# Two 2 KB vectors loaded as one descriptor each, with one-row matmuls making their columns, in a single-core decode step

## The chip, the cores and the metric

The kernel runs on one core of one Trainium2 chip. The metric is the device time of one execution in microseconds (us). Before the change it was 440.36 us, the median of three runs (440.32 to 440.46). Profiles are of one execution each. Where this text says "the profile", "the trace", "the timeline" or "the windows", it means views of such an execution. PE is the matmul engine, DVE the vector engine, ACT the scalar engine, POOL the GpSimd engine and SP the engine that issues most loads.

## The reference, cut to what matters

The reference is one decode step: adaLN modulation from `c`, attention of 32 query heads over a cache of 4 key heads and 65,536 positions, and a gated feed-forward block.

```python
mod = (silu(c) @ w_mod).reshape(1, 6, 1, 1024)        # c: (1, 1024), w_mod: (1024, 6144)
sa, ca, ga, sb, cb, gb = (mod[:, i] for i in range(6))
h = layernorm(x) * (1 + ca) + sa                      # x: (1, 1, 1024)
x = x + ga * attention(h, k_cache, v_cache, wq, wo)   # caches: (1, 4, 65536, 128) each
h = layernorm(x) * (1 + cb) + sb
x = x + gb * ((gelu(h @ w_gate) * (h @ w_up)) @ w_down)
```

All data is bf16. The weights and caches are 185.6 MB. The two vectors `c` and `x`, which the change is about, are 2 KB each.

## The kernel before

SP streams the weights and caches through ten slots of SBUF, the on-chip memory that the engines compute from. (PSUM, below, is the memory that PE writes its results to.) A descriptor is one contiguous piece of a load. In the trace each descriptor is a packet, and each of the 16 DMA engines that takes part in a load adds a packet of 4 bytes at its end, the completion. Before the change, ACT's queue loads `c` and `x` at the start. Each is wanted as columns, element `8 p + k` in partition `p`, so each load has 128 descriptors of 16 bytes. `x` is loaded a second time as eight rows of 256 bytes, which one matmul turns into a second column layout, `x_nat`.

```python
def emit_all():
    act.dma_start(c_in[:, :], c[0].rearrange("(p k) -> p k", p=P)).then_inc(c_sem, 16)
    act.dma_start(x_in[:, :], A_x[0, 0].rearrange("(p k) -> p k", p=P)).then_inc(x_sem, 16)
    act.dma_start(x_row[:, :], A_x[0, 0].rearrange("(j p) -> j p", p=P)).then_inc(in_sem, 16)
    # ... (cut) SP issues w_mod (8 loads), wq (4), then keys, values and the other weights
    # ... (cut) POOL: identities, small fills, and then the large one:
    v_zero = GP.done(pool.memset(kt_sb[:, 1, :, :], 0.0))
    # ... (cut) DVE: fills of s_pad, h_pad, o_pad
    AC.wait((c_sem, 16))
    v_th = AC.done(act.activation(th_col[:, :], c_in[:, :], ACT.Tanh, scale=0.5))
    DVE.wait(v_th)
    v = DVE.done(dve.tensor_scalar(sg_col[:, :], th_col[:, :], 0.5, 0.5, ALU.mult, ALU.add))
    DVE.wait(v, v_pads, (c_sem, 16))
    v_s = DVE.done(dve.tensor_tensor(s_pad[:, :, 0], c_in[:, :], sg_col[:, :], ALU.mult))   # silu(c)
    # ... (cut) PE: the layernorm's sums, then w_mod against s_pad, chunk by chunk
```

## Time and profile before

| | before |
|---|---|
| median time | 440.36 us |
| DMA: bytes, mean rate | 185.89 MB, 424 GB/s |
| PE busy, share of the span | 80% |
| packets on the queue of `c` and `x` | 304 |
| `s_pad` (silu of `c`) ready | 12.0 us |
| first w_mod matmul | 12.86 us |

The first lines are from the page of the kernel before: the busy share of the DMA engines in 40 equal slices, in tenths, what they moved, and the packets by queue. Queue q1 is SP's, q10 is ACT's.

```profile
DMA  8999999999999999999999999999999999999995
GB/s 332 427 435 428 430 429 432 432 433 425 430 445 420 453 414 455 408 445 438 410 448 415 445 419 442 427 435 432 430 437 424 439 423 433 432 427 431 424 425 237
DMA packets 11957, 185.89 MB, mean 424 GB/s; under 512 B 1568, under 2 KB 1568, under 8 KB 1952
...
q1 hardware_dynamic: 11632, 185.61, 98.8%
...
q10 hardware_dynamic: 304, 0.01, 0.0%
...
DMA 60%; PE 35%; DVE 2%; issue 1%; SPq 1%; ACT 1%; POOL 0%
```

The DMA engines are busy in 8 or 9 tenths of every slice but the last, and the rate stays between 408 and 455 GB/s except in the first slice and the last. The last line is the chain of waits by engine: 60% is DMA. So the span is a start, a stream at a fixed rate, and a tail. The 304 packets of q10 (264 descriptors and 40 completions; the 272 in the prediction below is a slip) carry 0.01 MB, and their recorded time rounds to 0.0% of the span.

The next lines are from the timeline before: start in us, duration in us, engine, line, operation, output and inputs, and in brackets the idle time before and what ended it.

```profile
4.75 6.95 POOL L341 MEMSET kt_sb<- 128x8192 bf16 x1
...
6.69 5.03 DVE L356 TENSOR_SCALAR sg_col<-th_col 128x8 f32<-128x8 f32 x1
...
11.76 0.20 DVE L358 TENSOR_TENSOR s_pad<-c_in,sg_col 128x8 bf16<-128x8 bf16 x1
...
12.86 4.78 PE L392 MATMUL kt_ps<-slots,s_pad 128*32 128x512 bf16 x36
...
18.16 1.04 PE L392 MATMUL kt_ps<-slots,s_pad 128*32 128x512 bf16 x12 [0.52 <-DMA slots<-in_w_mod_dram]
...
433.51 2.91 PE L372 MATMUL b<-u_col,slots 128*128 128x1 bf16 x96 [3.01 <-DMA slots<-in_B_w_down_dram]
```

`sg_col` has 8 elements in each partition and takes 5.03 us, until POOL's memset ends at 11.70 us. It ends with the memset and not with the landing of `c`, whose tanh had started at 5.01 us. PE then works off three w_mod chunks (36 matmuls) without a wait. At 18.16 us it waits for DMA for the first time, and it does so for each later chunk.

### The profile page before, as it was taken

The page shows a single profiled execution, that of the slowest core. Times are in us where ns is not written, and L with a number is a line of the kernel's source. Part 1 is how long each engine was busy: PE and PEld are TensorE (multiplying, and loading weights), DVE is VectorE, ACT ScalarE, POOL GpSimd, SP SyncE. Part 2 cuts the span into 40 slices and gives each one's busy share as a digit, 9 for nine tenths or more (in the row PEclk, how much of TensorE's full clock was granted, in tenths as well). Part 3 has the DMA queues.
Part 4 walks back from the last instruction along what each step waited for, and adds up shares of the span by engine and source line. Part 5 has one row for each costly group of instructions (what it writes and reads, how often), then busy time and mean ns, then how long its engine had stood idle before and what let it go on. Part 6 is the DMA issues. An engine that isn't in the chain of part 4 may idle for free.

```text
span 438.8 us, 15336 instructions
## 1 busy us (share of the span) xinstructions
PE 351.7 (80%) x7107; PEld 318.4 (73%) x7107; DVE 176.2 (40%) x300; ACT 146.4 (33%) x553; POOL 11.7 (3%) x25
## 2 busy tenths in 40 slices
PE   0547449998989889898799989999989999557554
PEld 0214139998989879798799989899988999434234
DVE  4102013545444644455444466345563365142100
ACT  1000001343435634344613553444654434600000
POOL 8100000000000000000000000000000000000000
PEclk9955555959777986869955899556995597659855
DMA  8999999999999999999999999999999999999995
GB/s 332 427 435 428 430 429 432 432 433 425 430 445 420 453 414 455 408 445 438 410 448 415 445 419 442 427 435 432 430 437 424 439 423 433 432 427 431 424 425 237
DMA packets 11957, 185.89 MB, mean 424 GB/s; under 512 B 1568, under 2 KB 1568, under 8 KB 1952
## 3 DMA queue, kind: packets, MB, share of 16 engines
q1 hardware_dynamic: 11632, 185.61, 98.8%
q8 instruction: 13, 0.21, 0.2%
q10 hardware_dynamic: 304, 0.01, 0.0%
q14 instruction: 8, 0.07, 0.0%
HBM read 185.60 MB, written 0.00 MB: 423 GB/s over the span
## 4 chain that ended last, share of the span: by engine, by line
DMA 60%; PE 35%; DVE 2%; issue 1%; SPq 1%; ACT 1%; POOL 0%
DMA slots<-in_A_v_cache_dram 39%; PE kt_ps L561 18%; DMA slots<-in_A_k_cache_dram 10%; DMA slots<-in_B_w_down_dram 7%; PE b L625 7%; PE sc_ps L581 6%; DMA slots<-in_w_mod_dram 4%; PE kt_ps L392 2%; PE b L605 1%; SPq L234 1%; PE b L372 1%; ACT p_sb L691 1%; PE b L595 1%; DVE kt_sb L751 0%; PE sc_ps L453 0%
## 5 line engine op out<-in xcount | busy, mean ns | idle before, releaser
L561 PE MATMUL kt_ps<-ident,slots 128*128 128x128 bf16 x2048 | 179.5, 258 | 11.0 <-DMA slots<-in_A_k_cache_dram 10.3
L561 PEld LDWEIGHTS kt_ps<-ident,slots 128*128 128x128 bf16 x2048 | 154.9, 118 | 12.7 <-issue 9.8
L660 DVE COPY kt_sb<-kt_ps 128x2048 bf16<-128x2048 bf16 x96 | 117.6, 1225 | 108.6 <-PE kt_ps L561 108.5
L660 ACT ACTIVATE kt_sb<-kt_ps 128x2048 bf16<-128x2048 bf16 x32 | 60.1, 1877 | 183.3 <-PE kt_ps L561 183.3
L625 PE MATMUL b<-p_sb,slots 128*128 128x8 bf16 x2176 | 75.8, 168 | 20.6 <-DMA slots<-in_A_v_cache_dram 11.2
L625 PEld LDWEIGHTS b<-p_sb,slots 128*128 128x128 bf16 x2176 | 69.8, 100 | 23.3 <-DMA slots<-in_A_v_cache_dram 12.3
L691 ACT ACTIVATE p_sb<-sc_ps,mneg 128x64 bf16<-128x64 f32 x256 | 83.5, 560 | 3.9 <-DVE mneg L686 3.9
L691 ACT ACTIVATION_READ_ACCUMULATOR p_sb<-sc_ps,mneg 128x1 f32 x256 | 77.1, 365 | 0.0
L581 PE MATMUL sc_ps<-q_buf,kt_sb 128*128 128x8 bf16 x2112 | 69.9, 167 | 0.5 <-issue 0.5
L581 PEld LDWEIGHTS sc_ps<-q_buf,kt_sb 128*128 128x128 bf16 x2112 | 67.9, 100 | 0.6 <-issue 0.6
L392 PE MATMUL kt_ps<-slots,h_pad 128*32 128x512 bf16 x176 | 17.1, 510 | 14.3 <-DMA slots<-in_A_wq_dram 6.3
L684 DVE TENSOR_REDUCE mg<-b 8x1 f32<-8x128 f32 x32 | 8.9, 279 | 37.1 <-PE b L595 37.1
L679 DVE TENSOR_REDUCE m_col<-sc_ps 128x8 f32<-128x512 f32 x32 | 21.8, 681 | 4.7 <-PE sc_ps L581 4.7
L392 PEld LDWEIGHTS kt_ps<-slots,h_pad 128*32 128x32 bf16 x176 | 5.0, 112 | 24.1 <-DMA slots<-in_A_wq_dram 8.3
L392 PE MATMUL kt_ps<-slots,s_pad 128*32 128x512 bf16 x96 | 12.5, 553 | 9.3 <-DMA slots<-in_w_mod_dram 9.3
L392 PEld LDWEIGHTS kt_ps<-slots,s_pad 128*32 128x32 bf16 x96 | 3.6, 119 | 17.3 <-DMA slots<-in_w_mod_dram 12.6
L605 PE MATMUL b<-negi,mg 8*128 8x8 f32 x66 | 15.8, 309 | 0.0
L605 PEld LDWEIGHTS b<-negi,mg 8*128 8x128 f32 x66 | 12.7, 239 | 2.2
L453 PEld LDWEIGHTS sc_ps<-identf,kt_sb 128*128 128x128 f32 (+1 forms) x48 | 7.6, 204 | 8.2 <-DVE kt_sb L774 4.3
L453 PE MATMUL sc_ps<-identf,kt_sb 128*128 128x128 f32 (+1 forms) x48 | 9.1, 352 | 4.5 <-DVE kt_sb L774 2.4
L686 DVE COPY mneg<-b 128x8 f32<-128x8 f32 x32 | 5.3, 167 | 18.1 <-PE b L605 18.1
L372 PE MATMUL b<-u_col,slots 128*128 128x1 bf16 x224 | 6.6, 165 | 6.5 <-DMA slots<-in_B_w_down_dram 5.9
(97 smaller groups left out, 84.9 us busy)
## 6 DMA issues: line engine op xcount, KB each, us to landing
slots<-in_A_k_cache_dram SPq DMA_DIRECT2D x16, 4096.0 KB, 20.3
slots<-in_A_v_cache_dram SPq DMA_DIRECT2D x32, 2048.0 KB, 26.5
slots<-in_w_mod_dram SPq DMA_DIRECT2D x8, 1536.0 KB, 17.5
slots<-in_A_wq_dram SPq DMA_DIRECT2D x4, 2048.0 KB, 35.2
slots<-in_A_wo_dram SPq DMA_DIRECT2D x4, 2048.0 KB, 32.5
slots<-in_B_w_gate_dram SPq DMA_DIRECT2D x4, 1792.0 KB, 21.9
slots<-in_B_w_up_dram SPq DMA_DIRECT2D x4, 1792.0 KB, 23.6
slots<-in_B_w_down_dram SPq DMA_DIRECT2D x3, 2048.0 KB, 29.1
```

Of the source, the lines that this page charges most:

```text
L372: ins = pe.matmul(bank[:, j:j + 1], view[:, kk, j * P:(j + 1) * P], rhs[:, k0 + kk:k0 + kk + 1], start=first, stop=True, skip_group_check= ...
L392: ins = pe.matmul(out, pad[:, k, :], jb.view[:, kk, c0:c0 + ROW], start=k <= last_k[0], stop=k >= last_k[1], skip_group_check=True,)
L453: ins = pe.transpose(dst[:, i * w:i * w + n], src[:, a], identf[0:src.shape[0], 0:n])
L561: ins = pe.transpose(kt_ps[:, half * 2048 + t * P:half * 2048 + (t + 1) * P], j_k[i - i % KU].view[:, i % KU * CH + b * TB + t, :], ident[ ...
L581: ins = pe.matmul(sc_ps[:, base + n * REP:base + (n + 1) * REP], kt_sb[:, j % 2, n, :], q_buf[:, j % SITES, :], start=True, stop=True,)
L605: ins = pe.matmul(b6[:, 256:256 + REP], mg8[:, j % 2:j % 2 + 1].to_broadcast([REP, P]), negi[:, :], start=True, stop=True,)
L625: ins = pe.matmul(b7[:, s * REP:(s + 1) * REP], j_v[j].view[:, n, :], p_sb[:, s, n, :], start=(n == 0), stop=(n == CH - 1),)
L660: ev[i % SITES][b].done(act.activation(dst, src, ACT.Copy) if E_ is AC else dve.tensor_copy(dst, src))
L679: m1[s].done(dve.tensor_reduce(m_col[:, j % 2, :].unsqueeze(2), scv, AX.X, ALU.max))
L684: m2[s].done(dve.tensor_reduce(mg8[:, j % 2:j % 2 + 1], b6[0:REP, 32:32 + P], AX.X, ALU.max))
L686: v_mc[j] = DVE.done(dve.tensor_copy(mneg[:, j, :], b6[:, 256:256 + REP]))
L691: ins = act.activation(p_sb[:, s, :, h], scv[:, h, :], ACT.Exp, bias=mneg[:, j, h:h + 1], scale=scale, accum_out=z_all[:, j, h:h + 1],)
```

## The change

The intent is to get rid of 256 descriptors of 16 bytes (and eight of 256 bytes) in the first microseconds. `c` and `x` come as one row each in a single partition, one 2 KB descriptor each. Matmuls with a contraction of one row turn strided slices of that row into columns in PSUM, and DVE copies them out.

```diff
-        act.dma_start(c_in[:, :], c[0].rearrange("(p k) -> p k", p=P)).then_inc(c_sem, 16)
-        act.dma_start(x_in[:, :], A_x[0, 0].rearrange("(p k) -> p k", p=P)).then_inc(x_sem, 16)
-        act.dma_start(x_row[:, :], A_x[0, 0].rearrange("(j p) -> j p", p=P)).then_inc(in_sem, 16)
+        act.dma_start(c_row, c).then_inc(c_sem, 16)
+        act.dma_start(x_row, A_x[0]).then_inc(x_sem, 16)
 ... (cut)
-        AC.wait((c_sem, 16))
-        v_th = AC.done(act.activation(th_col[:, :], c_in[:, :], ACT.Tanh, scale=0.5))
+        PE.wait(t1, (c_sem, 16))
+        for j in range(KD):
+            ins = pe.matmul(b7[:, j:j + 1], c_row[:, j:D:KD], ident[0:1, 0:1], start=True, stop=True)
+        v_cp = PE.done(ins)
+        PE.wait((x_sem, 16))
+        for j in range(KD):
+            pe.matmul(b6[:, j:j + 1], x_row[:, j:D:KD], ident[0:1, 0:1], start=True, stop=True)
+            ins = pe.matmul(
+                b6[:, KD + j:KD + j + 1], x_row[:, j * P:(j + 1) * P], ident[0:1, 0:1], start=True, stop=True)
+        v_xp = PE.done(ins)
+        DVE.wait(v_cp)
+        v_c = DVE.done(dve.tensor_copy(c_col[:, :], b7[:, 0:KD]))
+        AC.wait(v_c)
+        v_th = AC.done(act.activation(th_col[:, :], c_col[:, :], ACT.Tanh, scale=0.5))
+        DVE.wait(v_xp)
+        v_x = DVE.done(dve.tensor_copy(x_col[:, :], b6[:, 0:KD]))
+        v_x = DVE.done(dve.tensor_copy(x_nat[:, :], b6[:, KD:2 * KD]))
 ... (cut: sg_col as before; s_pad reads c_col in place of c_in; the old x_row matmul and x_nat copy go)
```

The rows lie in a part of `kt_sb` that nothing else uses until w_mod is done.

More of the change, by code (lines that the diff above doesn't have):

```diff
@@ L120, in bass_adaLN_cond__gqa_block_cached__geglu_ffn__decode_kernel @@
     sp, pe, dve, act, pool = nc.sync, nc.tensor, nc.vector, nc.scalar, nc.gpsimd
-    in_sem = nc.alloc_semaphore("in_sem")
     c_sem = nc.alloc_semaphore("c_sem")
@@ L138, in bass_adaLN_cond__gqa_block_cached__geglu_ffn__decode_kernel @@
     halfneg = sb("halfneg", [P, 1])
-    x_row = sb("x_row", [KD, P], dt.bfloat16)
-    c_in = sb("c_in", [P, KD], dt.bfloat16)
-    x_in = sb("x_in", [P, KD], dt.bfloat16)
+    c_col = sb("c_col", [P, KD])
     s_pad = sb("s_pad", [P, KD, QD], dt.bfloat16)
@@ L175, in bass_adaLN_cond__gqa_block_cached__geglu_ffn__decode_kernel @@
     row_m = ktf(0)[:, 0:4 * ROW]
+    c_row = kt_sb[0:1, 0, 0:KD, :].rearrange("p a b -> p (a b)")
+    x_row = kt_sb[0:1, 0, KD:2 * KD, :].rearrange("p a b -> p (a b)")
     row_q = ktf(0)[:, 4 * ROW:6 * ROW]
@@ L352, in emit_all @@
             v_pads = DVE.done(dve.memset(a[:, :, :], 0.0))
-        AC.wait((c_sem, 16))
-        v_th = AC.done(act.activation(th_col[:, :], c_in[:, :], ACT.Tanh, scale=0.5))
+        PE.wait(t1, (c_sem, 16))
[15 more added lines that the diff above has]
+        v_x = DVE.done(dve.tensor_copy(x_nat[:, :], b6[:, KD:2 * KD]))
         DVE.wait(v_th)
         v = DVE.done(dve.tensor_scalar(sg_col[:, :], th_col[:, :], 0.5, 0.5, ALU.mult, ALU.add))
-        DVE.wait(v, v_pads, (c_sem, 16))
-        v_s = DVE.done(dve.tensor_tensor(s_pad[:, :, 0], c_in[:, :], sg_col[:, :], ALU.mult))
-        DVE.wait((x_sem, 16))
-        v_x = DVE.done(dve.tensor_copy(x_col[:, :], x_in[:, :]))
+        DVE.wait(v, v_pads)
+        v_s = DVE.done(dve.tensor_tensor(s_pad[:, :, 0], c_col[:, :], sg_col[:, :], ALU.mult))
         def col_matvec(bank, jobs, rhs, ready, nblk):
@@ L460, in quads @@
             return t.rearrange("p (n g y) -> p n g y", n=n, g=w // QD)[:, :, :, 0]
-        PE.wait(t1, (in_sem, 16))
-        v_xt = PE.done(pe.matmul(b6[:, 0:KD], x_row[:, :], ident[0:KD, 0:KD], start=True, stop=True))
         hn1, v_hn1 = ln_norm(x_col[:, :], v_x, 16)
@@ L503, in rest_of_mod @@
             dve.tensor_copy(ga_nat[:, :], nv[:, 0, :])
-            dve.tensor_copy(gb_nat[:, :], nv[:, 1, :])
-            DVE.wait(v_xt)
-            DVE.done(dve.tensor_copy(x_nat[:, :], b6[:, 0:KD]))
+            DVE.done(dve.tensor_copy(gb_nat[:, :], nv[:, 1, :]))
         def place_2(b0, n):
```

## The prediction

> **What bounds the kernel now.** The DMA engines. The page shows a DMA share of 9 tenths or more in every slice but the first and last, 185.9 MB at a mean of 424 GB/s; in 5 us windows the rate stays near 430 GB/s from 3 to 430 us. Issue to landing takes 20 to 35 us (DMA issues), so the queue always holds several MB. The chain of waits is 60% DMA. PE is second (80% busy, mean granted clock 0.73), but what it releases late only shortens a long backlog. So time = start-up + bytes / rate + tail. Bytes and tail (last w_down chunk at 433.5 us, then about 5 us) don't change.
>
> **What the change removes.** The queue of c and x has 304 packets: 272 descriptors and completions. In the first 32 us they take 0.5% of the 16 engines: about 0.16 us of the stream. The windows agree: about 420 GB/s from 3 to 12 us, with these packets, against about 427 GB/s from 12 to 20 us, which is 0.15 us. The ramp (124, 222, 246 GB/s in the half microseconds from 1.5 to 3 us) may hide another 0.1 to 0.2 us.
>
> Landing gets sooner: c lands 4.3 us after its issue, x 8.2 us, x_row at 10.5 us. The Trainium skill ("DMA: Bandwidth & Descriptors", "Queues, rings and completion order") says each engine takes turns between queues, packet by packet. The trace agrees: 19 small packets per engine, alternating with 12 KB rows (0.46 us each at 27 GB/s per engine), make about 9 us. With one descriptor each I estimate landings at about 3 us (c) and 4 us (x).
>
> **What it adds.** 24 single-column matmuls (0.06 to 0.17 us each, PE idle until 10.5 us), and three PSUM copies of about 0.17 us on DVE before s_pad.
>
> **How much is critical.** Almost nothing of the latency. s_pad is ready at 12.0 us not because of c but because one DVE instruction, sg_col (0.5 * tanh + 0.5), starts at 6.69 us and lasts 5.03 us, until POOL's 6.95 us memset of kt_sb ends at 11.70. The Trainium skill ("SBUF — State Buffer", practical consequences) says a VectorE instruction in a 2-port mode blocks fully while GpSimd holds the shared pair. That instruction stays, with the same operands, so it still ends at about 11.7 us and s_pad comes at about 12. The new copies run in the wait (PSUM sources). Even that date is off the path: PE catches up with w_mod at 17.6 us and waits for the chunk that lands at 18.2, and from there for DMA.
>
> So only 0.15 to 0.4 us of freed DMA time reaches the end: **440.1 us**, range 439.4 to 440.8, mostly run-to-run and chip-to-chip spread. Chances: faster by over 2% 0.01, within 2% 0.98, slower 0.01.
>
> **What would show it.** Right: the queue of c and x falls to under 50 packets; sg_col starts at 7 to 8 us and still ends at about 11.7; s_pad at 11.8 to 12.2; first w_mod matmul at 12.3 to 13; the w_mod chunk of 18.16 us and the last w_down chunk (433.5 us) both 0.1 to 0.4 us sooner; DMA share unchanged. Wrong: s_pad moves by microseconds and the span follows, or the span moves while w_mod's landings do not.
>
> **What would make it wrong.** The single-partition landings queueing behind w_mod on one engine for over 10 us; the granted clock shifting so that PE empties the DMA backlog; the start of the w_mod stream moving by more than the 0.4 us allowed.

## The result, and the profile after

The changed kernel took 440.06 us (median of six runs, 439.85 to 440.20) against 440.44 us of the kernel before (six runs, 440.32 to 440.66). The ratio is the mean time of one kernel's runs over that of the other's in the same rounds, so it is not quite the ratio of those medians: 0.9991, with a 95% interval of 0.9978 to 1.0003. That is "the same" at the 2% that counts here. The interval includes 1, so these rounds alone don't show that the 0.38 us between the medians is real.

From the page after, the lines that answer to those above:

```profile
DMA packets 11659, 185.90 MB, mean 424 GB/s; under 512 B 1267, under 2 KB 1267, under 8 KB 1653
...
q1 hardware_dynamic: 11632, 185.61, 98.9%
...
q10 hardware_dynamic: 4, 0.00, 0.0%
...
DMA 60%; PE 34%; issue 2%; DVE 2%; SPq 1%; ACT 1%; POOL 0%
```

The 304 packets of q10 have become 4, a data packet and a completion for each load. SP's stream (q1) is the same. The timeline after:

```profile
2.45 0.63 PE L353 MATMUL b<-ident,kt_sb 1*128 1x1 bf16 x8 [2.45 <-DMA kt_sb<-in_c_dram]
...
4.75 6.95 POOL L339 MEMSET kt_sb<- 128x8192 bf16 x1
...
6.52 0.22 PE L357 MATMUL b<-ident,kt_sb 1*128 1x1 bf16 x1 [3.44 <-DMA kt_sb<-in_A_x_dram]
...
7.61 4.12 DVE L369 TENSOR_SCALAR sg_col<-th_col 128x8 f32<-128x8 f32 x1
...
11.76 0.19 DVE L371 TENSOR_TENSOR s_pad<-c_col,sg_col 128x8 bf16<-128x8 f32 x1
...
12.65 4.60 PE L403 MATMUL kt_ps<-slots,s_pad 128*32 128x512 bf16 x36
...
17.94 1.04 PE L403 MATMUL kt_ps<-slots,s_pad 128*32 128x512 bf16 x12 [0.69 <-DMA slots<-in_w_mod_dram]
...
433.47 2.85 PE L383 MATMUL b<-u_col,slots 128*128 128x1 bf16 x96 [3.04 <-DMA slots<-in_B_w_down_dram]
```

`c` is there by 2.45 us, yet `sg_col` still ends at 11.73 us, with the memset, and `s_pad` starts at 11.76 us in both kernels. The w_mod chunk that PE first waits for is 0.22 us sooner. At the last w_down chunk the two profiled runs differ by only 0.04 us. A difference of 0.4 us is not to be read off one pair of profiles at the end of the span: the profiled run of the kernel before took 440.15 us, faster than 31 of the 33 timed runs of that kernel (440.11 to 440.96).

One thing went the other way. The matmuls of the last of the eight w_mod chunks started at 33.82 us in place of 32.79 us. It was the same in later profiles (33.68 us in the repeat, 33.55 us with the two loads swapped), but not where only `c` was changed (32.51 us), so it seems to come with the change of `x`'s loads. The cause is open. The chunk is not on the path: it came 1.0 us later in a kernel that is not slower.

### The profile page after: what moved, and what is told of

Same layout as the page of the kernel before. It is cut to its first block, busy times and chain, and to the rows that moved or that the text cites. A ratio compares the mean times of both kernels' runs of the same rounds, so it can differ in the third digit from the quotient of the medians.

```text
span 438.8 us, 15381 instructions
## 1 busy us (share of the span) xinstructions
PE 344.4 (78%) x7130; PEld 310.8 (71%) x7130; DVE 175.1 (40%) x301; ACT 146.4 (33%) x553; POOL 11.7 (3%) x25
## 3 DMA queue, kind: packets, MB, share of 16 engines
q1 hardware_dynamic: 11632, 185.61, 98.9%
## 4 chain that ended last, share of the span: by engine, by line
DMA 60%; PE 34%; issue 2%; DVE 2%; SPq 1%; ACT 1%; POOL 0%
DMA slots<-in_A_v_cache_dram 39%; PE kt_ps L568 17%; DMA slots<-in_A_k_cache_dram 10%; DMA slots<-in_B_w_down_dram 7%; PE b L632 6%; PE sc_ps L588 6%; DMA slots<-in_w_mod_dram 4%; PE kt_ps L403 2%; PE b L612 1%; SPq L233 1%; PE b L383 1%; ACT p_sb L698 1%; PE b L602 1%; DVE kt_sb L758 0%; PE sc_ps L464 0%
## 5 line engine op out<-in xcount | busy, mean ns | idle before, releaser
L568 PE MATMUL kt_ps<-ident,slots 128*128 128x128 bf16 x2048 | 171.9, 251 | 12.8 <-issue 7.9
L568 PEld LDWEIGHTS kt_ps<-ident,slots 128*128 128x128 bf16 x2048 | 148.3, 114 | 14.4 <-issue 9.9
L632 PEld LDWEIGHTS b<-p_sb,slots 128*128 128x128 bf16 x2176 | 68.8, 99 | 29.0 <-DMA slots<-in_A_v_cache_dram 17.6
L588 PEld LDWEIGHTS sc_ps<-q_buf,kt_sb 128*128 128x128 bf16 x2112 | 66.9, 99 | 1.5 <-issue 1.4
L612 PE MATMUL b<-negi,mg 8*128 8x8 f32 x66 | 14.9, 296 | 0.0
L783 ACT ACTIVATE kt_sb<-kt_ps 96x512 f32<-96x512 f32 (+1 forms) x3 | 1.8, 594 | 30.6 <-PE kt_ps L403 30.6
```

What stands on the lines that cost most here:

```text
L568: ins = pe.transpose(kt_ps[:, half * 2048 + t * P:half * 2048 + (t + 1) * P], j_k[i - i % KU].view[:, i % KU * CH + b * TB + t, :], ident[ ...
L588: ins = pe.matmul(sc_ps[:, base + n * REP:base + (n + 1) * REP], kt_sb[:, j % 2, n, :], q_buf[:, j % SITES, :], start=True, stop=True,)
L612: ins = pe.matmul(b6[:, 256:256 + REP], mg8[:, j % 2:j % 2 + 1].to_broadcast([REP, P]), negi[:, :], start=True, stop=True,)
L632: ins = pe.matmul(b7[:, s * REP:(s + 1) * REP], j_v[j].view[:, n, :], p_sb[:, s, n, :], start=(n == 0), stop=(n == CH - 1),)
```

## The experiments

**Is the 0.4 us real?** The changed kernel again, with no edit.

> The changed kernel unaltered, to learn how firm the first difference of 0.38 us is. Theory A (the DMA engines are freed of about 300 small packets, which costs them 0.16 us of stream by the profile): 0.1 to 0.4 us faster than before, with the interval below 1. Rival N (the 0.38 us is noise of the runs): a difference of either sign under 0.2 us. Rival L (the earlier c and x matter): no prediction of its own here.

Measured: 440.03 us (439.89 to 440.06, five runs) against 440.50 us of before (440.27 to 440.96, nine runs); ratio 0.9989, interval 0.9975 to 1.0002. That is 0.47 us, a little more than the packet theory's 0.1 to 0.4 us, and the interval still just includes 1, which that theory had not expected. Over the whole study the changed kernel ran eleven times, median 440.03 us, range 439.85 to 440.20. The kernel before ran 33 times, median 440.48 us, and three of its runs lie at or below 440.20. So a difference of about 0.45 us is well supported by these runs together, and 0.1% is its size. Each run of the experiments also lists the core's span, from its first instruction to its last, to 0.1 us. Its median is 439.1 us for the kernel before (27 runs) and 438.7 us for the changed one (11 runs), so the difference lies inside the span.

**Seven more sets of the removed loads.** The dose is raised where it can't touch the early chain: on the changed kernel, after tanh.

```diff
+        for i in range(7):     # ACT queue, after tanh; extra: [P, 14, KD] bf16
+            act.dma_start(extra[:, 2 * i, :], c[0].rearrange("(p k) -> p k", p=P)).then_inc(ex_sem, 16)
+            act.dma_start(extra[:, 2 * i + 1, :], A_x[0, 0].rearrange("(p k) -> p k", p=P)).then_inc(ex_sem, 16)
 ... (cut)
+        sp.wait_ge(ex_sem, 224)  # at the very end
```

> The changed kernel plus seven more sets of the removed 16-byte loads (14 DMAs, 1,792 descriptors, 2,016 packets with completions) into a spare tile, issued after tanh, so that c, x and s_pad keep their dates. Theory A with the packets' recorded time (0.16 us for 304 packets): 1.1 us slower than the changed kernel; if instead the whole 0.38 us was packet cost: 2.5 us slower. Rival N or a saving from the start-up ramp or from latency alone: 0 to 0.2 us slower, since these loads begin at 7 us, after the ramp, and nobody waits for them but the end.

Measured: 442.03 us (441.93 to 442.25), 2.00 us over the changed kernel of the same rounds; ratio to before 1.0035, interval 1.0022 to 1.0049. The windows (us from the start; then busy time and count of each engine, granted PE clock, DMA share, GB/s) of the changed kernel in those rounds:

```profile
7.00:20.00 13.00, 7.16 (x55) 2.70 (x53) 5.58 (x11) 0.04 (x1) 5.25 (x2) 1.00 1.02 435
20.00:40.00 20.00, 9.47 (x60) 3.41 (x64) 1.80 (x4) 1.02 (x1) 0.00 (x0) 0.55 1.01 430
40.00:60.00 20.00, 11.67 (x96) 5.58 (x88) 1.51 (x6) 0.60 (x1) 0.00 (x0) 0.50 1.04 444
```

And of the kernel with seven more sets:

```profile
7.00:20.00 13.00, 5.88 (x55) 2.39 (x53) 5.61 (x11) 0.05 (x1) 5.28 (x2) 1.00 0.99 406
20.00:40.00 20.00, 9.36 (x56) 3.33 (x56) 1.22 (x1) 1.02 (x1) 0.00 (x0) 0.56 1.02 420
40.00:60.00 20.00, 12.17 (x97) 5.71 (x96) 2.09 (x9) 0.60 (x1) 0.00 (x0) 0.50 1.02 430
```

The ACT queue's line in the page of that kernel (packets, MB, share of 16 engines):

```profile
q10 hardware_dynamic: 2020, 0.03, 0.3%
```

The DMA share stays at 1, but the rate falls from 435 to 406 GB/s, from 430 to 420 and from 444 to 430, while small packets are in the engines. Worked out as lost bytes over the rate, that is 0.87 + 0.47 + 0.63 = 1.97 us. That this is so close to the 2.00 us is partly luck: about 500 of the 2,020 packets came only between 60 and 85 us, and against the first profile of the changed kernel (431, 431 and 442 GB/s) the same sum gives 1.8 us. A count that needs no windows: by 100 us SP's queue had moved 41.19 MB, against 41.83 and 41.98 MB in the two profiles of the changed kernel, which at 430 GB/s is 1.5 to 1.8 us. The core's span grew from 438.7 to 440.6 us. Nobody waits for these loads but the end of the kernel, so this is a cost of the stream, not of latency. It is about 1.0 us for 1,000 packets, or 16 ns of one engine for each packet (2.00 us x 16 engines / 2,016). That lies between the two forecasts of the packet theory (1.1 and 2.5 us). The profile records 0.3% of 16 engines for them, about 1.3 us: less than they cost.

**The same extra sets, one descriptor each.** In each of the 14 extra DMAs the destination is one row of 2 KB in a partition of its own.

```diff
+        for i in range(7):     # kt_sb[.., 48:56, :] is not in use yet
+            act.dma_start(kt_sb[2 * i:2 * i + 1, 0, 6 * KD:7 * KD, :].rearrange("p a b -> p (a b)"), c).then_inc(ex_sem, 16)
+            act.dma_start(kt_sb[2 * i + 1:2 * i + 2, 0, 6 * KD:7 * KD, :].rearrange("p a b -> p (a b)"), A_x[0]).then_inc(ex_sem, 16)
 ... (cut)
+        DVE.wait((ex_sem, 224))  # before attention
```

> The same seven extra sets with the same bytes, but one 2 KB descriptor for each (14 DMAs, 28 packets). Theory A (the count of packets is what costs): within 0.15 us of the changed kernel. Rival D (each DMA, or its bytes, is what costs): as slow as the kernel with seven extra sets of small descriptors.

Measured: 440.29 us (440.00 to 440.41), 0.26 us over the changed kernel and 1.74 us under the kernel with the same bytes in small descriptors. So it is the many small packets that cost, and not the bytes or the number of DMAs. But 0.26 us is more than the 0.15 us that the theory allowed, which the next run was for.

**The same 14 DMAs with 16 bytes each.** The edit is the one above with `[:, 0:KD]` on both sides.

> The same 14 extra DMAs as in the run with seven sets of one 2 KB descriptor each, but of 16 bytes each (28 packets again). That run was 0.26 us over the changed kernel, where its 28 packets explain 0.03. If the excess is a cost of each DMA: 0.2 to 0.3 us again. If it is the 28 KB that all go through one of the 16 engines (1.04 us of that engine at 27 GB/s, estimated): within 0.1 us of the changed kernel (440.03 to 440.08).

Measured: 440.27 us (440.19 to 440.36), 0.24 us over the changed kernel's 440.03 us of the earlier rounds (the kernel before was at 440.48 here and 440.50 there; this run and the last two experiments below were on another chip than the repeat of the changed kernel). So the bytes don't matter. By its size the 0.24 us looks like a cost of each DMA, but the record shows that it is not lost in the stream: the core's span has a median of 438.7 us in this run, in the one before it and in the changed kernel. What grew is the part of the time outside the span: 1.52 to 1.63 us here and 1.40 to 1.60 us in the run before, against 1.26 to 1.44 us in all eleven runs of the changed kernel. What that is, no view shows. So a price for each DMA is not shown. By the spans, the seven small sets cost 1.9 us: about 0.9 us for 1,000 packets, or 15 ns of one engine for each.

**Half of the change.** `c` comes as one row; `x` keeps its two old loads.

```diff
 # the kernel before, with
-        act.dma_start(c_in[:, :], c[0].rearrange("(p k) -> p k", p=P)).then_inc(c_sem, 16)
+        act.dma_start(c_row, c).then_inc(c_sem, 16)
 # and the eight one-row matmuls, the copy to c_col, and tanh and s_pad reading c_col
```

> Only c comes as one descriptor; x keeps its two small-descriptor loads. The queue of c and x should hold about 162 packets in place of 304. Theory A (packet cost, about 1.0 us per 1,000 packets by the run with seven extra sets): 0.15 us faster than before (0.05 to 0.25), so about 0.15 us slower than the whole change. Rival C (the saving comes from c's earlier start-up alone, in the first 2 us of the stream): the whole 0.4 us. Rival X (it comes from x's loads): none.

Measured: 440.25 us (440.02 to 440.32), 0.24 us under the before of its rounds (440.49) and 0.22 us over the changed kernel; ratio 0.9992, interval 0.9979 to 1.0006. q10 had 162 packets. About half the packets, and by the medians about half the saving (by the median spans, 438.8 us between 439.1 and 438.7, three quarters): it looks like neither the whole nor nothing. But the sizes are within the spread of the runs, so this run speaks for the packet theory without ruling the rivals out, and it fixes no price.

**`s_pad` four microseconds sooner.** POOL's large memset is moved behind `s_pad`.

```diff
-        v_zero = GP.done(pool.memset(kt_sb[:, 1, :, :], 0.0))
 ... (cut)
         v_s = DVE.done(dve.tensor_tensor(s_pad[:, :, 0], c_col[:, :], sg_col[:, :], ALU.mult))
+        GP.wait(v_s)
+        v_zero = GP.done(pool.memset(kt_sb[:, 1, :, :], 0.0))
```

> The changed kernel with POOL's 6.95 us memset moved after s_pad, so that nothing holds sg_col: s_pad should be ready at about 8 us in place of 11.9, and the first w_mod matmul should start at 8.5 to 9. Theory A (the stream is DMA-bound and this date has slack): the span within 0.15 us of the changed kernel; the matmuls of the fourth w_mod chunk still start at 17.9. Rival L (the early chain is critical): up to 3 us faster.

Measured: 440.07 us (439.85 to 440.26), against 440.03. Its timeline:

```profile
7.39 0.16 DVE L368 TENSOR_SCALAR sg_col<-th_col 128x8 f32<-128x8 f32 x1
7.59 0.19 DVE L370 TENSOR_TENSOR s_pad<-c_col,sg_col 128x8 bf16<-128x8 f32 x1
...
8.47 3.92 PE L404 MATMUL kt_ps<-slots,s_pad 128*32 128x512 bf16 x24
...
14.17 1.89 PE L404 MATMUL kt_ps<-slots,s_pad 128*32 128x512 bf16 x12 [1.77 <-DMA slots<-in_w_mod_dram]
...
17.88 1.89 PE L404 MATMUL kt_ps<-slots,s_pad 128*32 128x512 bf16 x12 [1.82 <-DMA slots<-in_w_mod_dram]
```

With nothing running on POOL, `sg_col` takes 0.16 us in place of 4.12, which shows that the memset had held it. `s_pad` is ready at 7.78 us, the first w_mod matmul starts at 8.47 us in place of 12.65, and PE then waits for DMA from the third chunk on. The fourth chunk still starts at 17.9 us and the span stays. Four microseconds of latency removed at the head were worth nothing.

**`s_pad` ten microseconds later.**

```diff
+        for _ in range(4):
+            DVE.wait(DVE.done(dve.memset(kt_sb[:, 0, 2 * KD:CH, :], 0.0)))   # about 10 us on DVE
         DVE.wait(v, v_pads)
         v_s = DVE.done(dve.tensor_tensor(s_pad[:, :, 0], c_col[:, :], sg_col[:, :], ALU.mult))
```

> The changed kernel with s_pad made about 10 to 13 us late by four dependent DVE memsets of a region not yet in use. Theory A (this date has slack behind the backlog of loads): the first w_mod matmul starts at 22 to 26 us in place of 12.7, PE works the landed chunks off, and the span is within 0.2 us of the changed kernel. Rival L (the early chain is critical): about 10 us slower.

Measured: 440.08 us (440.03 to 440.26, four runs). Its timeline:

```profile
21.76 0.19 DVE L373 TENSOR_TENSOR s_pad<-c_col,sg_col 128x8 bf16<-128x8 f32 x1
...
22.65 7.49 PE L405 MATMUL kt_ps<-slots,s_pad 128*32 128x512 bf16 x84
...
33.66 1.04 PE L405 MATMUL kt_ps<-slots,s_pad 128*32 128x512 bf16 x12 [3.52 <-DMA slots<-in_w_mod_dram]
...
433.40 2.84 PE L385 MATMUL b<-u_col,slots 128*128 128x1 bf16 x96 [3.22 <-DMA slots<-in_B_w_down_dram]
```

PE starts 10.0 us later, runs 84 matmuls of seven chunks without a wait, and still waits 3.5 us for the eighth. Ten microseconds of delay cost nothing, though the layernorm of `x`, which comes next on DVE, was held as long. Together with the run before, and with the one below in which `c` and `x` swap places (440.06 us in one look), this leaves the landing dates of `c` and `x` no part in the 0.4 us.

**Why `x` landed at 6.5 us.** I had estimated 4. Counts of q10 packets in windows that end at 5, 5.5, 5.75 and 6.25 us of the changed kernel, with q1's for the third:

```profile
q10 hardware_dynamic: 2, 0.00, 0.5%
...
q10 hardware_dynamic: 2, 0.00, 0.4%
...
q1 hardware_dynamic: 117, 1.44, 69.9%
q10 hardware_dynamic: 3, 0.00, 0.5%
...
q10 hardware_dynamic: 4, 0.00, 0.5%
```

`c`'s two packets come in the first 2.25 us. The third packet, `x`'s data, appears between 5.5 and 5.75 us, when the first w_mod load (128 rows, eight for each engine) is nearly through. Two runs ask whether it is the place in the queue. In the first, the two loads change places.

```diff
-        act.dma_start(c_row, c).then_inc(c_sem, 16)
         act.dma_start(x_row, A_x[0]).then_inc(x_sem, 16)
+        act.dma_start(c_row, c).then_inc(c_sem, 16)
```

> The two row loads change places in the ACT queue: x first, then c. In the changed kernel c landed by 2.4 us and x only at 6.5 us, against my estimate of 4. If the second load is held up by what the same engine is already doing for w_mod (theory P, position): c now lands at about 6.2 to 6.5 us and x by 2.4. If it is something of x itself (rival Y): x still at 6.5. Either way the span is within 0.3 us of the changed kernel, since sg_col waits for POOL until 11.7 us.

Measured: 440.06 us in one look (state unknown). PE's matmuls for `c` in its timeline:

```profile
6.35 0.63 PE L353 MATMUL b<-ident,kt_sb 1*128 1x1 bf16 x8 [6.35 <-DMA kt_sb<-in_c_dram]
```

Now `c` is the late one, at 6.35 us, so it is the place. In the second run the first w_mod chunk is cut into four DMAs with rows of 3 KB.

```diff
-            sp.dma_start(j.view, j.src).then_inc(j.tok[0], 16)
+            n = j.view.shape[-1] // j.cuts          # cuts: 4 for the first w_mod chunk, else 1
+            for q in range(j.cuts):
+                cols = (slice(None), slice(None), slice(q * n, (q + 1) * n))
+                sp.dma_start(*((j.view, j.src) if j.cuts == 1 else (j.view[cols], j.src[cols]))).then_inc(j.tok[0], 16)
```

> The first w_mod chunk is loaded by four DMAs with rows of 3 KB in place of one with rows of 12 KB, all else as in the changed kernel. Theory P (x's descriptor comes up only after the w_mod DMA ahead of it has gone through its engine): that DMA is now a quarter as long, so x lands at 3 to 4.5 us. Rival R (x is taken after one 12 KB row, or after a fixed time): x stays at 6 to 6.5 us, or lands about 0.5 us after c. Span within 0.5 us of the changed kernel: 48 completion packets more.

Measured: 441.09 us in one look. The first matmul on `x`:

```profile
4.18 0.22 PE L361 MATMUL b<-ident,kt_sb 1*128 1x1 bf16 x1 [1.20 <-DMA kt_sb<-in_A_x_dram]
```

With shorter w_mod DMAs ahead, `x` lands at 4.18 us in place of 6.52 (3.96 us in the profile of the repeat below). So the second load on ACT's queue waited for w_mod DMAs that were issued about when it was, and for longer when they were longer. Where it is held, in the making of descriptors or in the engine, no view here shows.

**The cut chunk again.**

> The one look at the first w_mod chunk in four DMAs with rows of 3 KB showed 441.09 us, 1.0 us over the changed kernel, for 432 packets more. Repeated to learn its size. At the small packets' price (1.0 us per 1,000): 0.43 us over the changed kernel. If the look holds: 1.0 us, more than twice that price, so that something other than the packets is lost there, such as the first rows' ramp.

Measured: 441.22 us (440.98 to 441.31, five runs), ratio to before 1.0014, interval 1.0001 to 1.0028. It is 1.19 us over the changed kernel, for 432 packets more (q1 had 12,064 in place of 11,632). That is 2.8 us for 1,000 packets, nearly three times the price of the small ones (by the spans, 439.8 against 438.7 us, 2.5 us for 1,000). So there is no single price for a packet. Most of the loss is early: the fourth chunk's matmuls start at 18.97 us in place of 17.94. Why it is so large is open.

**Fewer and longer rows for w_mod.** If packets cost so much, would merging large ones pay?

```diff
-        head = [8, 9, 0, 1, 2, 4, 3, 5, 6, 7, 8, 9]
-        j_mod = [(plan_load(wmod_v[:, k:k + 1, :], flat(1, M6), head[k]), k, 1) for k in range(KD)]
+        head = [8, 0, 2, 4, 6, 7, 8, 9]
+        j_mod = [(plan_load(wmod_v[:, k:k + 2, :], flat(2, M6), head[k // 2], nslot=2), k, 2) for k in range(0, KD, 2)]
```

> The changed kernel with w_mod in four loads with rows of 24 KB in place of eight with rows of 12 KB: 576 packets fewer, all of the large kind. If every packet costs what the small ones do (about 1.0 us per 1,000): 0.55 us faster than the changed kernel. If the time of a large row's packet is hidden behind its own bytes, since w_mod already streams at 435 GB/s from 7 to 20 us: within 0.15 us of the changed kernel. The later first landing (3 MB, near 9 us) should not matter, as the run with s_pad 10 us late showed.

Measured: 440.26 us (440.11 to 440.42), 0.23 us over the changed kernel's 440.03 of the earlier rounds, so somewhat outside the 0.15 us of the second theory and on the other side of the first. Here too the excess is outside the span (1.65 to 1.82 us); the span's median is 438.6 us, 0.1 us under the changed kernel's, which fits the second theory. So 576 fewer packets gained at most 0.1 us. The rate was higher from 7 to 20 us (446 GB/s against 435 in the repeat of the changed kernel) but lower before (344 against 367 from 2 to 7 us) and after (424 against 430 from 20 to 40 us). By the median device time no kernel was faster than the changed one.

The doses side by side (medians; q10 packets from the profile; the span is the core's):

| kernel | extra DMAs | q10 packets | span, us | us | over the changed kernel |
|---|---|---|---|---|---|
| changed | 0 | 4 | 438.7 | 440.03 | |
| 14 DMAs of 16 bytes more | 14 | 32 | 438.7 | 440.27 | 0.24 |
| 14 DMAs of one 2 KB row more | 14 | 32 | 438.7 | 440.29 | 0.26 |
| `c` alone changed | 1 | 162 | 438.8 | 440.25 | 0.22 |
| before | 1 | 304 | 439.1 | 440.48 | 0.45 |
| seven small sets more | 14 | 2,020 | 440.6 | 442.03 | 2.00 |

## Why the prediction was right

- **The bound: right.** I called the kernel a start, a DMA stream and a tail. The runs with `s_pad` 4.2 us sooner and 10.0 us later, both within 0.05 us of the changed kernel, show that PE's early dates don't count.
- **The instruction that holds `s_pad`: right.** `sg_col` started at 7.61 us and ended at 11.73 us, as said. With the memset moved it took 0.16 us.
- **The size: right in sum, with one term mis-sized and one not settled.** I took 0.15 us for the removed packets, from their recorded share, and 0.1 to 0.2 us for a slow ramp. The packet term was too small: at the price of the run with seven sets, 300 packets cost about 0.3 us. The ramp term is not settled: by 4 us SP's queue had moved 0.71 MB in the one profile before and 0.72 to 0.79 MB in four profiles with the changed start, and by 6 us 1.54 MB against 1.54 to 1.59, which at 430 GB/s is 0 to 0.2 us and 0 to 0.1 us. By 16 us, with the small packets through, it was 5.76 MB against 5.86 to 5.90, or 0.2 to 0.3 us: there the saving can be seen in the stream itself. 440.1 us was predicted and 440.06 us measured, which is in part luck, as the packet term was half of what it should have been. And the range of 439.4 to 440.8 us would have held with no change at all. The median difference of 0.45 us over all runs is a little above the 0.4 us that I allowed as freed time, while the range in us held.
- **The remainder: open.** Of the 0.45 us, about 0.3 us is the packets at that price. The rest, about 0.15 us, could be the ramp, spread of the runs, a higher price of packets in the first microseconds, or something about the third load that went. These runs don't tell.
- **The landing of `x`: wrong.** The step that failed is "With one descriptor each I estimate landings at about 3 us (c) and 4 us (x)". It rested on strict turns, packet by packet, between the queues. That fits the kernel before, where between 3 and 4 us q10 went from 88 to 122 packets and q1 from 24 to 58, 34 each, and it gave `c`'s landing well enough (by 2.45 us). It doesn't fit the changed kernel, where `x` came at 6.5 us, behind a whole w_mod DMA: the queueing that the prediction had named as a risk, if only for over 10 us. It cost nothing, since `sg_col` was held until 11.7 us anyway.
- **Dates: mostly right.** `s_pad` at 11.95 us and the first w_mod matmul at 12.65 us were in their ranges, and the fourth w_mod chunk was 0.22 us sooner. The last w_down chunk was only 0.04 us sooner in the first profile and 0.16 us (433.35 us) in the profile of the repeat.

## What to carry to other kernels

When a stream of loads keeps the DMA engines busy from end to end, small descriptors beside it cost what they take from that stream (here about 1 us for 1,000 of 16 bytes), and how soon they land is worth nothing unless somebody waits for them at the end of a chain. Before counting on latency saved at the head of a kernel, look for what really holds the next instruction: here it was a memset on another engine. And a tenth of a per cent has to be shown by raising the dose, not by a pair of profiles.

## What the Trainium skill lacked or had wrong

- "DMA: Bandwidth & Descriptors", the closing note under "Rules for kernel authors", says that which is faster, a flat row or many partitions for the same bytes, has not been measured. Here `[128, 8]` against `[1, 1024]`, loaded beside a saturated stream, cost 2.00 us against 0.26 us for 14 loads of 2 KB (in the core's span, 1.9 us against nothing to 0.1 us). The row was not split over the engines: it made one data packet and one completion.
- The same page, section "Bandwidth", gives about 10.5 ns for each packet, measured on the GpSimd path. That is the time of one small DMA over all its packets, and not a measured cost of a packet beside a stream, which the page does not give. Here, on ACT's queue and beside a full stream, a packet of 16 bytes cost 15 to 16 ns of an engine. Rows of 3 KB in place of 12 KB cost more for each added packet (1.19 us for 432), and why is open.
- The same page, section "Queues, rings and completion order", has each engine take turns between queues at packets. The kernel before agrees (34 small packets and 34 rows between 3 and 4 us). That section does not say that a second small DMA of one queue can wait for a whole DMA of the other: `x` landed at 6.5 us, and at 4.2 us when the w_mod DMAs ahead had rows of a quarter of the length.
- The same page, section "Anatomy of one DMA", gives the time that one DMA takes from end to end on the GpSimd path, not what a nearly empty one takes from a full stream. Here 14 of them added 0.24 us to the device time and, to 0.1 us, nothing to the core's span; what the 0.24 us is stays open.
- "SBUF — State Buffer", section "Who interferes with whom", was right: `sg_col`, a one-input fp32 instruction from SBUF to SBUF, was held until POOL's memset ended (4.12 us) and took 0.16 us without it.
